# Bias masks for two key blocks at once in the tail rows, and one query load per head in the second half of the batch

## The chip, the cores and the metric

The kernel runs on one core of a Trainium2 chip. The metric is the device time of one execution in microseconds (us). The core has a matrix engine (PE, with its weight loads listed as PEld), a vector engine (DVE), a scalar engine (ACT), a general engine (POOL), and a queue (SP) from which all of this kernel's DMAs are issued. Each engine works through its instructions in the order in which they stand in its queue.

## What is computed

Attention with a learned relative bias, and then a two-layer network with a squared ReLU:

```python
# q, k, v: (4, 8, 576, 64); w1: (1, 32); b1: (32); w2: (32, 8)
scores = scale * np.matmul(q, k.transpose(0, 1, 3, 2))
psi_rel = np.log1p(np.abs(rel))                     # rel[i, j] = i - j
psi_i = np.log1p(np.maximum(pos[:, None], 1.0))
h = np.maximum((psi_rel / psi_i)[..., None] @ w1 + b1, 0.0)
scores = scores + (h @ w2).transpose(2, 0, 1)[None]
attn = np.exp(scores - max); attn = attn / (sum + 1e-09)
x = np.matmul(attn, v) as (2304, 512)
# network: w_in (512, 2048), w_out (2048, 512)
out = np.maximum(x @ w_in, 0.0) ** 2 @ w_out
```

## The kernel before

**Units.** The 576 query rows are cut into five chunks: four of 128 rows and a tail of 64 rows (`TAIL`, index 4). Heads go in pairs (`hp`, four of them). A unit is one batch, one pair of heads, one chunk. In the tail, the two heads of a pair share the 128 partitions, 64 rows each. The first 40 units are batches 0 and 1 (`b < AB`), by chunk: u0 to u7 are the tail chunk of the eight (batch, pair) combinations, u8 to u15 chunk 0, and so on. The last 40, u40 to u79, are batches 2 and 3, by (pair, batch), five chunks each, the tail last.

A unit runs `scores` (matmuls into the PSUM tile `sp`, then on DVE `t`, which adds the bias and takes the row extreme, then on ACT `p`, the exponential), two units later `transposes` (PE into `pp`, ACT copies to `pt`), then `values` (PE into `px`, copied to `xT`). `sp` has one buffer, `t` two, `p` three.

**Bias.** The bias of a chunk is made once, in 18 key blocks of 32 keys (`jb`), and is used by all batches. Because the bias is piecewise linear in the distance, `bias_mask` compares a window of a distance table with thresholds (`mask`, 128 partitions of 4 keys x 32 hidden units, 1024 two-byte elements each), and `bias_sum` multiplies the masks on PE by the weights `wmov` (16 matmuls per block, mask as the stationary operand of 128 columns, 64 columns moving) into a PSUM tile `bb`. ACT scales one half of it into `bt2`, DVE multiplies the other half by `xc` (the distances of that chunk, loaded by `load_xc`) into `bt1`, and POOL adds the two into `area`. In the tail a mask covers 64 rows and stands twice, for the two heads of a pair; for six of the 18 blocks (`MD`) DVE makes 64 columns and ACT copies them. The products are taken in two halves of 64 partitions. `bb`, `pp` and `px` share a ring of four PSUM buffers (`aux`), taken in the order of the program.

The tail's bias is made first. Between its blocks the program issues the loads of the eight (batch, pair) combinations of the first half, seven DMAs each: two of keys, four of queries (for each head the tail's 64 columns, L150, and the other 512, L151), one of values. After them it loads `xc` of chunk 0 (L573). The loop over units then makes `BO` blocks of the next chunk's bias beside the eight units of each chunk.

**The second half.** At unit 40 (`NA`) the loop loads keys and queries of the first three combinations of batches 2 and 3 (L637 to L639), then the first two of 16 tiles of `w_in` (`load_w`, L642 to L644, 512 KB each, two buffers). From unit 41 (`SC`) on, over ten units, each tile is scanned for its largest value (`scan_w`, DVE, L189) and the tile two further on is loaded into its buffer. The scans are held in program order on DVE. Later, `split_in` turns the tiles into pairs of two-byte parts beside the units, and then the network runs.

**Order.** The program is put into queues by a planner that simulates it with its own costs, so a change in one place can move instructions elsewhere.

Of the kernel before, what the change touches and what calls it, by code (L numbers as in the profile page):

```python
# [17 lines left out]
ALU = mybir.AluOpType  # L18
# [42 lines left out]
B1 = (2, 13, 8)  # L61
# [3 lines left out]
MD = 37449  # L65
K0 = 2
# [13 lines left out]
def attention_then_relu2_mlp(ctx: ExitStack, tc: tile.TileContext, q, k, v, cols, w_in, w_out, psi, xmat, dist, out):  # L80
# [65 lines left out]
    def load_q(b, hp):  # L146
        t = kq_p[-1].tile([128, S], F32, name="q1", tag="q1")
        for h in range(2):
            rows = slice(64 * h, 64 * h + 64)
            SP.dma_start(out=t[rows, 512:], in_=q[b, hp, TAIL, :, h, rows])  # L150
            SP.dma_start(out=t[rows, :512].rearrange("d (i m) -> d i m", i=TAIL), in_=q[b, hp, :TAIL, :, h].rearrange("i d m -> d i m"))  # L151
        q_t[b, hp] = t

# [182 lines left out]
    def bias_weights():  # L340
        ab = prep.tile([128, 2, H], F32, name="ab")
        part = prep.tile([128, 2, 2 * H], F16, name="part")
        eng = POOL if BW else DVE
        eng.memset(wmov, 0.0)
        for n in range(2):
            eng.tensor_scalar(out=ab[:, n], in0=col[:, 2:10], scalar1=(w1, b1)[n], scalar2=8.0, op0=ALU.mult, op1=ALU.mult)
        r = ab.rearrange("p a h -> p (a h)")

        pw = ps.tile([128, 512], F32, name="pw", tag="aux", bufs=4)
        sig, isig = power(r, pw[:, 0:1])  # L350
        eng.tensor_scalar(out=r, in0=r, scalar1=sig, scalar2=None, op0=ALU.mult)
        eng.tensor_copy(out=part[:, 0], in_=r)
        eng.tensor_tensor(out=part[:, 1], in0=r, in1=part[:, 0], op=ALU.subtract)
        wv = wmov.rearrange("p n (m j) -> p n m j", j=4)
        for jj in range(4):
            eng.tensor_copy(out=wv[32 * jj:32 * jj + 32, :, :, jj], in_=part[32 * jj:32 * jj + 32])
        return isig
# [3 lines left out]
    def bias_mask(ic, jb):  # L361
        m = prep.tile([128, 8, 128], F16, name="mask", tag="mask", bufs=MB)
        dup = ic == TAIL and (MD >> jb) & 1
        w = 64 if dup else 128
        base = sdist[:, 128 * ic + 548 - 32 * jb:]
        if ic < TAIL or dup:
            win = bass.AP(tensor=base.tensor, offset=base.offset, ap=[base.ap[0], [4, 8], [1, w]])
            th = theta[:, 128 * ic:128 * ic + w].unsqueeze(1)
            DVE.tensor_tensor(out=m[:, :, :w], in0=win, in1=th.to_broadcast([128, 8, w]), op=ALU.is_ge)  # L369
        else:  # L370
            win = bass.AP(tensor=base.tensor, offset=base.offset, ap=[base.ap[0], [4, 8], [0, 2], [1, 64]])
            th = theta[:, 512:].unsqueeze(1).unsqueeze(1).to_broadcast([128, 8, 2, 64])
            DVE.tensor_tensor(out=m.rearrange("p g (r i) -> p g r i", r=2), in0=win, in1=th, op=ALU.is_ge)
        if dup:
            ACT.copy(m[:, :, 64:], m[:, :, :64])
        mask_t[ic, jb] = m

    def bias_sum(ic, jb):
        m = mask_t.pop((ic, jb))
        bb = ps.tile([128, 512], F32, name="bb", tag="aux", bufs=4)  # L380
        for r in range(8):
            for n in range(2):
                PE.matmul(bb[:, 64 * (7 - r):64 * (8 - r)], lhsT=m[:, r], rhs=wmov[:, n], start=(n == 0), stop=(n == 1))  # L383
        t = prep.tile([128, H, 32], F32, name="bt1", tag="bt1", bufs=BB)
        s = prep.tile([128, H, 32], F32, name="bt2", tag="bt2", bufs=BB)
        xv = xc_t[ic][:, 32 * jb:32 * jb + 32].rearrange("p (g j) -> p g j", j=4).unsqueeze(1)
        bv = bb.rearrange("p (g a h j) -> p a h g j", g=8, a=2, h=H)
        tv = t.rearrange("p h (g j) -> p h g j", j=4)
        sv = s.rearrange("p h (g j) -> p h g j", j=4)
        js = slice(32 * jb, 32 * jb + 32)  # L390
        if ic < TAIL:
            ACT.activation(out=sv, in_=bv[:, 1], func=AF.Identity, scale=bscale)
# [4 lines left out]
            tw, sw = (y.rearrange("p (h e) j -> p h e j", e=2) for y in (t, s))  # L397
            POOL.tensor_tensor(out=dst, in0=tw, in1=sw, op=ALU.add)  # L398
        else:
            for r in range(2):  # L400
                rows = slice(64 * r, 64 * r + 64)
                bw = bb[rows].rearrange("p (g a h e j) -> p a e h g j", g=8, a=2, h=HP, e=2)
                ACT.activation(out=sv[rows, :HP], in_=bw[:, 1, r], func=AF.Identity, scale=bscale[rows])
                DVE.tensor_tensor(out=tv[rows, :HP], in0=bw[:, 0, r], in1=xv[rows].to_broadcast([64, HP, 8, 4]), op=ALU.mult)  # L404
            POOL.tensor_tensor(out=bias_t[:, 8::9, js], in0=t[:, :HP], in1=s[:, :HP], op=ALU.add)
# [4 lines left out]
    def scores(u):  # L410
# [11 lines left out]
        cols = slice(128 * ic, 128 * ic + 128 if ic < TAIL else S)  # L422

        for m, (x, h) in enumerate((x, h) for x in range(2) for h in (1, 0)):
            rows = slice(64 * h, 64 * h + 64)
            k0 = HALF * x + (64 if h and ic == TAIL else 0)
            out_t, to = (sps[h], slice(0, 128)) if ic < TAIL else (sps[0], rows)
# [114 lines left out]
    todo = [(ic, jb) for ic in chunks for jb in range(NJB)]  # L542
# [29 lines left out]
    bias_upto(NJB)  # L572
# [55 lines left out]
    for s in range(NU + TL + 1):  # L628
# [7 lines left out]
        for m, g in enumerate(groups[AB * HP:]):  # L636
            if s == max(first[g] - KL, NA):  # L637
                load_k(*g)
                load_q(*g)  # L639
            if s == max(first[g] - KL + TL + 1, NA - AB * HP + 2 + TL + m):  # L640
                load_v(*g)
        if s == SC - 1:  # L642
            load_w(ins[0])
            load_w(ins[1])  # L644
# [21 lines left out]
        if s < AB * HP * TAIL:  # L666
            n, r = divmod(s, AB * HP)
            bias_upto(NJB * (n + 1) + BO[r])
# [221 lines left out]
```

## Time and profile before

| | us |
|---|---|
| median of 3 runs | 798.25 |
| lowest, highest | 797.27, 798.29 |
| the profiled execution | 797.97 |
| its span from first to last instruction | 796.2 |

The profile is of one execution. Busy shares: PE 91%, PEld 72%, DVE 72%, ACT 57%, POOL 23%. Times in its views count from the start of the span, so what lies around the span is 1.77 us. The views used are the page's shares, the chain of work that ended last (each step followed back to what released it), timelines of one engine (start, length, line, operation, tiles and shapes, count, and in brackets the idle time before it with what ended it), sums by windows, and the list of waits. Matmul ends are modelled, so a group of many matmuls is read by the starts of what follows it. SPq is the issue of a DMA by the SP queue.

### The profile page before, as it was taken

The page shows a single profiled execution, that of the slowest core. Times are in us where ns is not written, and L with a number is a line of the kernel's source. Part 1 is how long each engine was busy: PE and PEld are TensorE (multiplying, and loading weights), DVE is VectorE, ACT ScalarE, POOL GpSimd, SP SyncE. Part 2 cuts the span into 40 slices and gives each one's busy share as a digit, 9 for nine tenths or more (in the row PEclk, how much of TensorE's full clock was granted, in tenths as well). Part 3 has the DMA queues.
Part 4 walks back from the last instruction along what each step waited for, and adds up shares of the span by engine and source line. Part 5 has one row for each costly group of instructions (what it writes and reads, how often), then busy time and mean ns, then how long its engine had stood idle before and what let it go on. Part 6 is the DMA issues. An engine that isn't in the chain of part 4 may idle for free.

```text
span 796.2 us, 17616 instructions
## 1 busy us (share of the span) xinstructions
PE 723.5 (91%) x7094; PEld 571.7 (72%) x7094; DVE 574.5 (72%) x1215; ACT 456.5 (57%) x940; POOL 186.4 (23%) x295
## 2 busy tenths in 40 slices
PE   5499999999988999979889899999989999999992
PEld 5456778787756676656677677878768887888881
DVE  7867778785666678898897979784845576557661
ACT  5757777777655678888676656664442233224220
POOL 1444333232210023342223324250400021000000
PEclk7869999999989999999999999999999999999997
DMA  7610000000376522301231143001010001000100
GB/s 203 191 60 18 3 16 2 3 2 2 105 239 232 189 85 85 111 28 54 80 107 54 67 146 107 28 22 59 26 54 1 1 1 54 1 1 1 54 2 27
DMA packets 27990, 50.14 MB, mean 63 GB/s; under 512 B 5252, under 2 KB 13444, under 8 KB 27908
## 3 DMA queue, kind: packets, MB, share of 16 engines
q1 hardware_dynamic: 27908, 49.01, 18.8%
q8 instruction: 56, 0.92, 0.5%
q14 instruction: 26, 0.21, 0.1%
HBM read 43.23 MB, written 5.77 MB: 62 GB/s over the span
## 4 chain that ended last, share of the span: by engine, by line
PE 50%; DVE 19%; ACT 8%; DMA 7%; SPq 6%; issue 5%; POOL 3%; DVEq 0%; ACTq 0%; POOLq 0%
PE y L766 16%; PE ha L717 8%; PE sp L428 7%; PE px L502 6%; PE hb L717 5%; PE pp L484 4%; PE bb L383 4%; DMA stage<-in_w_in 3%; DVE t L434 3%; ACT p L439 2%; SPq L150 2%; SPq L151 2%; DVE area L618 2%; DVE gl L747 1%; DVE wa L185 1%
## 5 line engine op out<-in xcount | busy, mean ns | idle before, releaser
L766 PE MATMUL y<-w,gh 128*128 128x512 f32 x576 | 177.9, 401 | 2.5 <-ACT gh L746 1.3
L717 PEld LDWEIGHTS <-area 128*128 128x128 f16 x1680 | 147.4, 99 | 42.5 <-issue 15.3
L439 ACT ACTIVATE p<-t,negm 128x576 f32<-128x576 f32 x144 | 111.2, 775 | 27.0 <-DVE negm L434 26.8
L434 DVE CUSTOM_DVE_ANT_0 t<-sp,area 128x576 f32<-128x576 f32 x144 | 104.1, 752 | 30.0 <-PE sp L428 21.3
L766 PEld LDWEIGHTS y<-w,gh 128*128 128x128 f32 x576 | 105.9, 190 | 24.9 <-ACT gh L746 2.9
L428 PE MATMUL sp<-k,q 64*128 64x288 f32 (+1 forms) x640 | 108.2, 447 | 15.0 <-DVE negm L434 11.4
L717 PE MATMUL ha<-area 128*128 128x256 f16 (+1 forms) x960 | 106.3, 266 | 9.0 <-DVE area L734 4.9
L766 PE MATMUL y<-w,gl 128*128 128x512 f32 x288 | 107.5, 397 | 1.1 <-DVE gl L747 1.1
L502 PE MATMUL px<-pt,v 128*64 128x128 f32 (+1 forms) x1600 | 96.6, 267 | 3.5 <-DVE xT L507 2.0
L485 ACT COPY pt<-pp 128x512 f32<-128x512 f32 x144 | 79.7, 582 | 32.0 <-PE pp L484 31.9
L502 PEld LDWEIGHTS px<-pt,v 128*64 128x64 f32 x1600 | 79.2, 137 | 19.7 <-issue 8.2
L484 PE MATMUL pp<-ident,p 128*128 128x128 f32 x576 | 84.5, 283 | 5.5 <-ACT pt L485 2.4
L428 PEld LDWEIGHTS sp<-k,q 64*128 64x128 f32 (+1 forms) x640 | 55.9, 182 | 41.1 <-DVE negm L434 15.3
L717 PE MATMUL hb<-area 128*128 128x256 f16 (+1 forms) x720 | 79.9, 262 | 1.4 <-DVE area L618 0.9
L484 PEld LDWEIGHTS pp<-ident,p 128*128 128x128 f32 x576 | 62.0, 142 | 22.8 <-issue 7.4
L398 POOL TENSOR_TENSOR area<-bt,bt 128x256 f32<-128x256 f32 x72 | 53.2, 763 | 81.9 <-DVE bt L393 81.9
L383 PE MATMUL bb<-wmov,mask 128*128 128x64 f16 x1440 | 52.6, 199 | 14.3 <-DVE bt L404 11.0
L766 PEld LDWEIGHTS y<-w,gl 128*128 128x128 f32 x288 | 53.8, 189 | 13.6 <-DVE gl L747 2.2
L383 PEld LDWEIGHTS <-mask 128*128 128x128 f16 x1440 | 48.2, 102 | 21.3 <-DVE bt L404 11.8
L369 DVE TENSOR_TENSOR mask<-sdist,theta 128x1024 f16<-128x1024 f16 (+1 forms) x78 | 49.7, 669 | 9.4 <-PE bb L383 9.4
L615 POOL TENSOR_TENSOR area<-xT 128x512 f32<-128x512 f32 (+1 forms) x17 | 22.8, 1344 | 143.2 <-DVE area L618 143.2
L747 DVE TENSOR_TENSOR gl<-area,gh 128x512 fp32r<-128x512 f32 (+1 forms) x40 | 30.2, 776 | 24.1 <-ACT gh L746 17.2
(153 smaller groups left out, 945.9 us busy)
## 6 DMA issues: line engine op xcount, KB each, us to landing
stage<-in_w_in SPq DMA_DIRECT2D x32, 512.0 KB, 4.2
stage<-in_w_out SPq DMA_DIRECT2D x16, 512.0 KB, 3.5
v<-in_v SPq DMA_DIRECT2D x16, 320.0 KB, 3.8
out<-o SPq DMA_DIRECT2D x18, 256.0 KB, 2.0
q<-in_q SPq DMA_DIRECT2D x32, 128.0 KB, 3.3
k<-in_k SPq DMA_DIRECT2D x16, 160.0 KB, 3.7
k<-in_k SPq DMA_DIRECT2D x16, 144.0 KB, 3.7
xc<-in_xmat SPq DMA_DIRECT2D x5, 288.0 KB, 3.6
```

What stands on the lines that cost most here:

```text
L369: DVE.tensor_tensor(out=m[:, :, :w], in0=win, in1=th.to_broadcast([128, 8, w]), op=ALU.is_ge)
L383: PE.matmul(bb[:, 64 * (7 - r):64 * (8 - r)], lhsT=m[:, r], rhs=wmov[:, n], start=(n == 0), stop=(n == 1))
L398: POOL.tensor_tensor(out=dst, in0=tw, in1=sw, op=ALU.add)
L428: mm = PE.matmul(out_t[to, x, :HALF], lhsT=qt[rows, cols], rhs=kt[rows, k0:k0 + HALF], start=True, stop=True)
L434: DVE.tensor_tensor_reduce(out=t.rearrange("p (x n) -> p x n", x=2), in0=sp[:, :, :HALF], in1=bias.rearrange("p (x n) -> p x n", x=2), sca ...
L439: ACT.activation(out=p[:, S * n:S * n + S], in_=t, func=AF.Exp, bias=negm[:, n:n + 1], scale=-1.0, accum_out=sums[:, 2 * ic + n:2 * ic + n ...
L484: PE.transpose(pp[:, 128 * c:128 * c + 128], p[:, k0:k0 + 128], ident)
L485: ACT.copy(pt[:, 4 * h:4 * h + 4], pp.rearrange("p (c m) -> p c m", c=4))
L502: PE.matmul(px[64 * h:64 * h + 64, :w], lhsT=vt[:, c, h], rhs=src, start=(c == 0), stop=(c == 4))
L717: PE.matmul(h[:, s, :w], lhsT=a, rhs=x, start=(k == 0), stop=(k == 5))
L747: DVE.tensor_tensor(out=gl, in0=g, in1=gh.bitcast(F32), op=ALU.subtract)
L766: PE.matmul(y, lhsT=a[:, slot, o:o + 128], rhs=x, start=((n, P) in firsts and f == 0 and m == 0), stop=((n, P) in lasts and f == 1 and m = ...
```

## The change

Three parts. In the tail, one mask now serves two key blocks: its 1024 elements are two narrow windows of 64 rows for neighbouring blocks, and nothing is doubled. The 18 blocks become nine pairs. Each narrow mask is loaded as a stationary operand of 64 columns, once for each head of a pair (`e`), into the upper or lower 64 partitions of `bb`, with 32 columns moving: 64 matmuls per pair of blocks in place of 32. The products on ACT and DVE and the add on POOL are then one operation per pair over all partitions. The order of heads in the weights changes to suit. In the second half, the queries of a head come in one DMA of 640 columns, the zero padding of the tail included, instead of two; `scores` reads the tail's columns at an offset for the second head. The first two loads of `w_in` are issued after the first and the second combination's keys and queries instead of after the third's. The counts `K0`, `B1` and the loop's targets are restated in pairs.

```diff
-B1 = (2, 13, 8)
+B1 = (2, 5, 8)
-MD = 37449
-K0 = 2
+K0 = 1
     def load_q(b, hp):
+        if b >= AB:
+            t = kq_p[-1].tile([128, NIC * 128], F32, name="q1", tag="q1")
+            for h in range(2):
+                SP.dma_start(out=t[64 * h:64 * h + 64].rearrange("d (i m) -> d i m", i=NIC), in_=q[b, hp, :, :, h].rearrange("i d m -> d i m"))
+            q_t[b, hp] = t
+            return
...
     def bias_mask(ic, jb):
...
+            base = sdist[:, 128 * ic + 548 - 32 * (jb + 1):]
+            win = bass.AP(tensor=base.tensor, offset=base.offset, ap=[base.ap[0], [4, 8], [32, 2], [1, 64]])
             th = theta[:, 512:].unsqueeze(1).unsqueeze(1).to_broadcast([128, 8, 2, 64])
+            out = m.rearrange("p g (x i) -> p g x i", x=2)
-        if dup:
-            ACT.copy(m[:, :, 64:], m[:, :, :64])
+        DVE.tensor_tensor(out=out, in0=win, in1=th, op=ALU.is_ge)
...
     def bias_sum(ic, jb):
...
-            for r in range(2):
-                rows = slice(64 * r, 64 * r + 64)
-                bw = bb[rows].rearrange("p (g a h e j) -> p a e h g j", g=8, a=2, h=HP, e=2)
-                ACT.activation(out=sv[rows, :HP], in_=bw[:, 1, r], func=AF.Identity, scale=bscale[rows])
-                DVE.tensor_tensor(out=tv[rows, :HP], in0=bw[:, 0, r], in1=xv[rows].to_broadcast([64, HP, 8, 4]), op=ALU.mult)
-            POOL.tensor_tensor(out=bias_t[:, 8::9, js], in0=t[:, :HP], in1=s[:, :HP], op=ALU.add)
+            wv = wmov.rearrange("p n (a e y) -> p n e a y", a=2, e=2)
+            for x in range(2):
+                for r in range(8):
+                    o = 256 * x + 32 * (7 - r)
+                    for n in range(2):
+                        for e in range(2):
+                            PE.matmul(
+                                bb[64 * e:64 * e + 64, o:o + 32].rearrange("p (a y) -> p a y", a=2),
+                                lhsT=m[:, r, 64 - 64 * x:128 - 64 * x], rhs=wv[:, n, e], start=(n == 0), stop=(n == 1),
+                            )
...
+            ACT.activation(out=sv.rearrange("p h (g j) -> p h g j", j=4), in_=bv[:, 1], func=AF.Identity, scale=bscale)
+            DVE.tensor_tensor(out=tv.rearrange("p h (g j) -> p h g j", j=4), in0=bv[:, 0], in1=xv.to_broadcast([128, HP, 16, 4]), op=ALU.mult)
+            POOL.tensor_tensor(out=bias_t[:, 8::9, 32 * jb:32 * jb + 64], in0=tv, in1=sv, op=ALU.add)
...
+            q0 = 128 * ic + (64 if h and ic == TAIL and b >= AB else 0)
+            cols = slice(q0, q0 + (128 if ic < TAIL else 64))
...
-    todo = [(ic, jb) for ic in chunks for jb in range(NJB)]
+    todo = [(ic, jb) for ic in chunks for jb in range(0, NJB, 2 if ic == TAIL else 1)]
...
             if s == max(first[g] - KL, NA):
                 load_k(*g)
                 load_q(*g)
+                if s == SC - 1 and m < 2:
+                    load_w(ins[m])
...
-        if s == SC - 1:
-            load_w(ins[0])
-            load_w(ins[1])
```

## Rows read from the trace of the kernel before

**Rows 1.** The page, part 1: busy us of each engine, share of span, instructions.
```profile
PE 723.5 (91%) x7094; PEld 571.7 (72%) x7094; DVE 574.5 (72%) x1215; ACT 456.5 (57%) x940; POOL 186.4 (23%) x295
```
**Rows 2.** Chain that ended last, 0 to 140 us: start, length, what.
```profile
2.59 0.59 SPq L137
...
40.27 0.60 SPq L143
40.92 3.62 DMA xc<-in_xmat
44.56 0.78 ACT xc L121
...
57.33 0.73 PE px L502 x20
58.06 1.51 PE bb L383 x48
```
**Rows 3.** Timeline of DVE, 0 to 50 us: the tail's masks, the first scores.
```profile
23.55 0.79 DVE L373 TENSOR_TENSOR mask<-sdist,theta 128x1024 f16<-128x1024 f16 x1
...
24.59 0.41 DVE L369 TENSOR_TENSOR mask<-sdist,theta 128x512 f16<-128x512 f16 x1
...
27.09 0.80 DVE L373 TENSOR_TENSOR mask<-sdist,theta 128x1024 f16<-128x1024 f16 x1
...
39.05 0.76 DVE L434 CUSTOM_DVE_ANT_0 t<-sp,area 128x576 f32<-128x576 f32 x1
```
**Rows 4.** Timeline of DVE, 44 to 100 us: products of chunk 0, first scores of u8.
```profile
46.07 1.08 DVE L393 TENSOR_TENSOR bt<-bb,xc 128x256 f32<-128x256 f32 x3
...
70.77 0.76 DVE L434 CUSTOM_DVE_ANT_0 t<-sp,area 128x576 f32<-128x576 f32 x1 [1.35 <-POOL area L398]
```
**Rows 5.** Timeline of PE, up to 207 us: bias products, scores, narrow stationary operands.
```profile
13.67 4.42 PE L383 MATMUL bb<-wmov,mask 128*128 128x64 f16 x80 [3.33 <-DVE wmov L356]
...
46.21 2.25 PE L428 MATMUL sp<-k,q 64*64 64x288 f32 x8 [0.97 <-DVE negm L434]
48.39 2.74 PE L383 MATMUL bb<-wmov,mask 128*128 128x64 f16 x48
...
56.14 1.19 PE L428 MATMUL sp<-k,q 64*64 64x288 f32 x8
...
204.67 0.41 PE L470 MATMUL ra<-rows,pick 27*64 27x128 bf16 x8
204.92 0.19 PE L470 MATMUL rt<-rows,pick 27*64 27x64 bf16 x2
```
**Rows 6.** Windows of 10 us: busy us (count) by engine, granted clock, DMA share, GB/s.
```profile
40.00:50.00 10.00, 8.17 (x55) 4.37 (x56) 4.63 (x12) 5.02 (x11) 3.44 (x7) 0.50 0.35 115
...
240.00:250.00 10.00, 7.97 (x87) 6.04 (x85) 6.57 (x19) 6.21 (x15) 0.97 (x5) 1.00 0.82 263
```
**Rows 7.** Timeline of the SP queue, 195 to 300 us: loads at unit 40 and after.
```profile
210.02 0.47 SPq L137 DMA_DIRECT2D k<-in_k  x1
...
211.18 0.60 SPq L150 DMA_DIRECT2D q<-in_q  x1
...
221.41 2.00 SPq L151 DMA_DIRECT2D q<-in_q  x1
223.51 1.02 SPq L172 DMA_DIRECT2D stage<-in_w_in  x2
...
263.88 1.73 SPq L150 DMA_DIRECT2D q<-in_q  x1
```
**Rows 8.** Timeline of DVE, 196 to 275 us: the first and the last scan.
```profile
227.74 0.69 DVE L189 TENSOR_REDUCE small<-stage 128x1 f32<-128x512 f32 x1 [3.60 <-DMA stage<-in_w_in]
...
269.96 0.69 DVE L189 TENSOR_REDUCE small<-stage 128x1 f32<-128x512 f32 x1 [1.46 <-DMA stage<-in_w_in]
```
**Rows 9.** Waits, 205 to 275 us: total us, times, longest.
```profile
DVE small L189 <- DMA stage<-in_w_in: 13.0, 10, 3.6
```
**Rows 10.** Chain that ended last, 140 to 420 us: a piece of `split_in`.
```profile
325.51 0.69 DVE zw L185
```

## What was predicted before the run

> **What bounds the kernel now.** The page's shares come first [rows 1]: PE is busy 91% of the span, so elsewhere a microsecond of another engine is mostly hidden. The change touches two stretches where PE is not the limit, so each is read for itself. For the first I read the chain of waits: from 2.59 to 40.9 us it runs through the issue of DMAs alone, 56 of them (8 combinations x 7) at about 0.65 us each, then through the load of `xc` for chunk 0, which lands at 44.54, and its scaling on ACT to 45.34 [rows 2]. Beside that chain DVE makes the tail's bias: three blocks repeat every 27.09 - 23.55 = 3.54 us, 1.18 us a block, and the first `t` runs at 39.05 [rows 3]. PE only runs in bursts there, and its granted clock is 0.50, the 1.2 GHz level, in the window from 40 to 50 us [rows 6]. From 48.39 PE works without a gap worth naming until u8's stage, where DVE's `t` stands at 70.77 [rows 4, 5]: that stretch is PE's.
>
> For the second I read SP's and DVE's timelines around unit 40. SP can issue from 210.02, when the memory of the first half's last unit is free, and needs until 223.4 for 18 loads of keys and queries; only then come the two loads of `w_in` [rows 7]. DVE stands still 3.60 us until the first has landed and scans it at 227.74; u42's `t` is queued behind that scan. The last scan is at 269.96 [rows 8]. In this stretch DVE waits 13.0 us for these loads [rows 9], and the DMA share is 0.82 at 240 to 250 us [rows 6]. It is a chain of loads into two buffers, not PE.
>
> **Tail's bias, work of each engine.** On DVE a pair of blocks cost 2 x 1.18 = 2.36 us. Now it costs one mask of 1024 elements, at most 0.79 [rows 3], and one product of 256 elements, 1.08 / 3 = 0.36 [rows 4]: 1.15. Nine pairs take 10.4 us in place of 21.2. The new window differs from the old wide one only in the step between its two halves, so I give it the same price. ACT loses six copies and three of every four products, POOL half its adds; neither was the limit and both get nothing.
>
> PE gets 576 matmuls in place of 288, each half as wide in stationary and moving columns. At 2.4 GHz a `bb` matmul takes 1.51 / 48 = 31.5 ns [rows 2]; half the moving columns, with two halves of the array side by side, would give 15.7 ns at the least. From above, `px` in the tail has the same stationary shape, also alternating between the halves, with 64 moving columns of four bytes: 0.73 / 20 = 36.5 ns [rows 2]. Nearest is `ra`, 64 two-byte stationary columns, alternating, 128 moving: 8 matmuls between the starts at 204.67 and 204.92, 31 ns [rows 5], and this one moves four times our columns. I take 24 ns, about midway between 15.7 and 31: 13.8 us (9.0 to 21.0). The first products ran at 4.42 / 80 = 55 ns, the lower clock level [rows 5]; those 4.4 us at half rate add 2.2. So the tail's bias is ready at 13.67 + 13.8 + 2.2 + 1.0 for the last product and add = 30.7 us (25.9 to 37.9), where `t` started at 39.05.
>
> **What that buys on the path.** Not 8 us, for the next thing late is `xc`: its load is behind the same 56 issues, so chunk 0's products still cannot start before 45.4. While they wait, their `bb` tiles hold all four `aux` buffers, and the first transposes stand behind them. With `p` three deep and `t` two, the tail units can get as far as p(u2), t(u4) and the score matmuls of u5. Before, they had got to p(u2), with sp(u3) at 46.21, right where chunk 0's work should have begun. So the gain is: the fifth `bb` can start at about 45.9 and not at 48.39, 2.5 us, and the score matmuls of u4 and u5 leave PE's gapless stretch, 2 x 1.19 = 2.4 [rows 5]. That is 4.9 at most; nothing at least, if the tail is ready only at 37.9 or if the planner does not use the window. I take 3.5, since DVE and ACT share the stretch and will not follow PE to the last. The time at u8 then carries over, as PE is full up to unit 40.
>
> **The loads at unit 40.** The order becomes: two loads of keys, two of queries, `w_in` 0, the same again, `w_in` 1, then the third combination. The first `w_in` load is issued after four issues of about 0.6 us, at 210.02 + 2.5 = 212.5 in before's time, not at 223.51: 11 us sooner [rows 7]. With the landing it took before (223.51 to 227.74, 4.2 us) it is there at 216.7; if the keys' and queries' traffic doubles that, at 221. Either is before DVE is free for it at about 224.1, which is 227.74 less the 3.60 of idling. What is moved behind it, the third combination's keys and queries, needs six fewer issues in all and still goes out by about 218.5 instead of 223.4; its units come ten units later. Nobody waits for that. The first scan, and with it u42's `t` and the load into the freed buffer, comes 3.6 us earlier (0 to 4.2). The 15 steps to the last scan took 269.96 - 227.74 = 42.2 us, 2.8 us each, paced by two buffers; I keep that pace. The first step also had a part that waited for the second tile, which now is there too: 0.6 more, so 4.2.
>
> **Query loads.** Each of the eight combinations saves two issues, 1.2 us of SP. In the first half nothing changes, since `load_q` branches on `b >= AB`. Late in the scans two query loads stand right ahead of the last tile's load, one of them 1.73 us [rows 7]. One issue of 0.6 us leaves that place: 0.6 (0 to 2.3). The 32 KB of padding for each combination is 256 KB, at 263 GB/s [rows 6] 1 us of traffic spread over 130 us: nothing.
>
> **The sum.** 3.5 + 4.2 + 0.6 = 8.3 us. Against the profiled execution: 797.97 - 8.3 = 789.7. The median of the runs is 0.3 above that execution, so 790.0. From the bounds alone: best 4.9 + 4.2 + 2.3 = 11.4, so 786.9; worst 798.25.
>
> **Rivals.** First, the tail's gain stays behind the load of `xc`: the planner lets DVE and PE wait in the same places as now, or the narrow matmuls cost 36.5 ns and the tail is ready at 37.9. Then 4.8 us remain, 793.5. For it: 45.34 is fixed by 56 issues that nothing shortens. Against it: sp(u3) demonstrably sat on PE at 46.21. It decides from a tail that is ready at 38, 1 us short of 39.05: (38 - 16.9) / 576 = 37 ns per matmul. The Trainium skill says in "TensorEngine Tiling (Array Packing)", under Restrictions, that column tiling switches off the fast weight load, and in "TensorE: Matmul & The Clock Gate", under LDWEIGHTS, that a load takes its columns / 1.2 in ns. By that, an estimate of 53 ns for 64 columns, the loads alone would take 31 us if the two halves' loads did not overlap, the tail would be ready near 47, and this rival would hold; `ra`'s 31 ns per matmul speaks for an overlap.
>
> Second, the scans are bound by bandwidth and not by their start: the share of 0.82 means that whatever lands earlier delays something else, and the last scan stays near 269. Then only 3.5 + 0.6 remain, 794.2. Against it: the 11 us ahead of the scans carry less traffic than that.
>
> Third, on the slower side: the planner places the pieces of `split_in` and `split_x` otherwise after 271 us, where PE is not full and DVE, ACT and POOL hand work to one another. A piece such as 0.69 us on DVE [rows 10] that moves ahead of a unit's `t` puts off the unit by as much. From 8.3 / 0.69 = 12 such places on it eats the gain; 15 of the 29 units from u51 on would be 10.4 us, so 790.0 + 10.4 = 800.4. For it: the planner sees new costs and new loads, and orders by its own model. Against it: that part of the program is the same, and it only starts earlier.
>
> Fourth, both gains fail and the change does nothing that counts: about 798.
>
> **How the numbers follow.** Forecast 0.47, first rival 0.18, second 0.14, third 0.12, fourth 0.09. The time is the likeliest's, 790.0. The range from 785.5 to 797.5 takes in the first two rivals and the best sum with some room for an order that happens to fit better; it leaves out the third and most of the fourth. A measurement of this kernel can tell about 0.2%, 1.6 us, from no change. The forecast and the first two rivals are faster, 0.79; within 0.2%: 0.09; slower: 0.12.
>
> **What would show it.** In the changed kernel's timelines: nine masks and nine products on DVE in the tail; the first `t` near 31 us; 64 narrow matmuls of a pair in about 1.5 us at the 2.4 GHz level; `xc` landing still near 44.5; PE's `bb` work starting again by 46 and u8's `t` near 67. Around unit 40, counted from SP's first key load: `w_in` 0 issued 2.5 us after it instead of 13.5, the first scan without its 3.6 us of waiting, the last scan about 55 us after that load instead of 60. From there on the stretch to the end should have the old length, about 526 us. The prediction is wrong if the matmuls take over 37 ns, if u8's `t` does not move, or if the last stretch changes its length by more than 2 us.

## The result and the profile after

The changed kernel is slower: median 803.33 us (802.03 to 807.0, six runs) against 797.34 us for the kernel before (795.53 to 798.29, six runs), ratio 1.0086, 95% interval 1.0067 to 1.0106. The profiled execution took 803.9 us, its span is 802.1 us, 5.9 more than before. Runs of one kernel spread by about 0.6% either way, so verdicts below go by ratios, and a trace, which is of one run, is used for where the time lies.

The page's shares [rows 1] hardly differ, and so don't tell where the 6 us lie:

```profile
PE 728.8 (91%) x7382; PEld 579.6 (72%) x7382; DVE 565.5 (70%) x1179; ACT 442.7 (55%) x907; POOL 185.7 (23%) x286
```

I therefore laid the two traces side by side by units: the first `t` of each unit on DVE's timeline, after minus before. That gives +10.2 us at u0, +7.1 at u8, +2.9 from u17 to u39, -0.7 at u50, +5.4 at u53 and the same to u79, +5.9 at the end. Three stretches thus have a sign of their own: **+2.9 up to u39, -3.7 from u39 to u50, +6.1 from u50 to u53**; the rest adds 0.6.

**Up to u39.** Timelines of the changed kernel at the end of the tail's bias: ACT (products of `bb`, scaling of `xc`), then DVE, then POOL:

```profile
29.15 0.48 ACT L411 ACTIVATE bt<-bb,small 128x256 f32<-128x256 f32 x1 [1.23 <-PE bb L403]
45.95 0.78 ACT L120 ACTIVATE xc<-xc,small 128x576 f32<-128x576 f32 x1 [16.33 <-DMA xc<-in_xmat]
46.63 0.45 ACT L411 ACTIVATE bt<-bb,small 128x256 f32<-128x256 f32 x1
...
47.12 0.42 DVE L412 TENSOR_TENSOR bt<-bb,xc 128x256 f32<-128x256 f32 x1 [15.04 <-ACT bt L411]
49.21 0.74 DVE L443 CUSTOM_DVE_ANT_0 t<-sp,area 128x576 f32<-128x576 f32 x1
...
30.19 0.74 POOL L413 TENSOR_TENSOR area<-bt,bt 128x256 f32<-128x256 f32 x1 [0.97 <-DVE bt L412]
47.62 1.11 POOL L413 TENSOR_TENSOR area<-bt,bt 128x256 f32<-128x256 f32 x1 [16.69 <-DVE bt L412]
```

Eight of nine pairs are added by 30.9. The ninth pair's product (L411, 46.63) stands behind the scaling of chunk 0's `xc` (L120) in ACT's queue. That scaling waits 16.3 us for the load, and with it wait the last product, DVE, POOL and every unit. In the kernel before, this scaling, at 44.56 [rows 2], stood behind the first exponentials, as its timeline of ACT shows:

```profile
40.17 0.78 ACT L439 ACTIVATE p<-t,negm 128x576 f32<-128x576 f32 x1
...
44.56 0.78 ACT L121 ACTIVATE xc<-xc,small 128x576 f32<-128x576 f32 x1 [0.73 <-DMA xc<-in_xmat]
```

In the changed program too it comes behind all of the tail's products; the planner put it in front of the last one.

**At unit 40.** SP's timeline, first loads, against [rows 7]:

```profile
212.95 0.47 SPq L136 DMA_DIRECT2D k<-in_k  x1
213.47 0.59 SPq L137 DMA_DIRECT2D k<-in_k  x1
214.10 1.68 SPq L149 DMA_DIRECT2D q<-in_q  x2
215.88 0.56 SPq L172 DMA_DIRECT2D stage<-in_w_in  x1
...
261.16 0.49 SPq L136 DMA_DIRECT2D k<-in_k  x1
261.71 0.59 SPq L137 DMA_DIRECT2D k<-in_k  x1
262.34 0.62 SPq L149 DMA_DIRECT2D q<-in_q  x1
263.37 0.33 SPq L172 DMA_DIRECT2D stage<-in_w_in  x1
263.75 0.62 SPq L149 DMA_DIRECT2D q<-in_q  x1
264.63 7.58 SPq L172 DMA_DIRECT2D stage<-in_w_in  x3
```

`w_in` 0 goes out 2.9 us after the first key load (before: 13.5), and the first scan runs at 226.51 without a wait. The last six lines hold the last two tiles (263.37 and 264.63), now 1.3 us apart and between the keys and queries of the fifth combination. In before they were issued 3.1 us apart, 262.65 and 265.71. DVE's timeline shows the last two scans [rows 8], PE's, below them, who waits:

```profile
269.42 0.69 DVE L189 TENSOR_REDUCE small<-stage 128x1 f32<-128x512 f32 x1 [3.20 <-DMA stage<-in_w_in]
271.16 0.69 DVE L189 TENSOR_REDUCE small<-stage 128x1 f32<-128x512 f32 x1 [0.86 <-DMA stage<-in_w_in]
...
270.36 2.40 PE L511 MATMUL px<-pt,v 128*64 128x128 f32 x20 [2.75 <-DVE xT L516]
273.80 2.29 PE L437 MATMUL sp<-k,q 64*128 64x288 f32 x8 [1.03 <-DVE small L217]
```

Windows of 5 us of the same stretch, columns as in [rows 6]:

```profile
265.00:270.00 5.00, 2.60 (x22) 1.74 (x17) 1.80 (x5) 2.75 (x7) 0.98 (x5) 0.95 0.90 240
270.00:275.00 5.00, 3.60 (x26) 3.01 (x28) 3.06 (x12) 1.63 (x4) 0.00 (x0) 0.50 0.66 210
275.00:280.00 5.00, 5.00 (x34) 3.67 (x31) 1.88 (x8) 2.27 (x6) 0.00 (x0) 0.52 0.04 13
280.00:285.00 5.00, 5.00 (x50) 3.54 (x48) 1.87 (x6) 2.26 (x6) 0.00 (x0) 1.00 0.00 0
```

The clock falls within PE's first wait (2.75 us, up to 270.36): the granted clock is 0.95 from 265 to 270 and then 0.50, the 1.2 GHz level, in the two windows from 270 to 280. The second wait (1.03 us) lies in that stretch. The matmul groups behind the waits take 2.40 and 2.29 us; in the kernel before, the groups of the same lines take 1.31 (at 269.53) and 1.24 (at 268.36). DVE's waits on the loads of `w_in` sum to 7.4 us from 205 to 275, where they were 13.0 [rows 9]: less in all, but now more than half of it at the last two scans.

The start of the last scan (271.16, before 269.96) divides the 6.1 us. Windows from u50's `t` to the last scan, and from there to u53's `t`, first of the kernel before, then of the changed one:

```profile
265.57:269.96 4.39, 4.39 (x50) 3.40 (x50) 2.32 (x8) 3.47 (x10) 0.00 (x0) 1.00 0.81 264
269.96:277.92 7.96, 6.79 (x78) 5.12 (x73) 5.01 (x20) 4.96 (x13) 0.00 (x0) 1.00 0.31 107
```
```profile
264.84:271.16 6.32, 3.55 (x33) 2.68 (x31) 2.27 (x7) 2.75 (x7) 0.99 (x5) 0.87 0.78 207
271.16:283.28 12.12, 11.09 (x74) 8.00 (x72) 4.92 (x19) 5.23 (x13) 0.00 (x0) 0.64 0.26 86
```

Up to the last scan 1.9 us are lost, in PE's wait. Behind it 4.2 us are lost: PE is busy for 11.09 us in place of 6.79 with about as many matmuls, at a mean clock of 0.64 in place of 1.00, and idle for no longer than before.

### The profile page after: what moved, and what is told of

It is laid out like the page before. It is cut to its first block, busy times and chain, and to the rows that moved or that the text cites. A ratio compares the mean times of both kernels' runs of the same rounds, so it can differ in the third digit from the quotient of the medians.

```text
span 802.1 us, 18086 instructions
## 1 busy us (share of the span) xinstructions
PE 728.8 (91%) x7382; PEld 579.6 (72%) x7382; DVE 565.5 (70%) x1179; ACT 442.7 (55%) x907; POOL 185.7 (23%) x286
## 4 chain that ended last, share of the span: by engine, by line
PE 56%; DVE 17%; DMA 6%; ACT 6%; SPq 5%; issue 5%; POOL 2%; DVEq 0%; ACTq 0%; POOLq 0%
PE y L774 18%; PE ha L725 8%; PE sp L437 7%; PE px L511 7%; PE pp L493 5%; PE hb L725 5%; PE bb L384 4%; DVE t L443 3%; DMA stage<-in_w_in 3%; DVE area L627 2%; SPq L156 1%; DMA stage<-in_w_out 1%; SPq L155 1%; ACT p L448 1%; DVE gl L755 1%
## 5 line engine op out<-in xcount | busy, mean ns | idle before, releaser
L437 PE MATMUL sp<-k,q 64*128 64x288 f32 (+1 forms) x640 | 104.3, 437 | 8.9 <-DVE negm L443 5.5
L511 PE MATMUL px<-pt,v 128*64 128x128 f32 (+1 forms) x1600 | 98.7, 271 | 5.0 <-DVE xT L516 2.7
L511 PEld LDWEIGHTS px<-pt,v 128*64 128x64 f32 x1600 | 81.1, 139 | 21.2 <-issue 7.4
L373 DVE TENSOR_TENSOR mask<-sdist,theta 128x1024 f16<-128x1024 f16 x81 | 56.0, 727 | 14.4 <-PE bb L403 8.2
L774 PEld LDWEIGHTS y<-w,gl 128*128 128x128 f32 x288 | 53.4, 188 | 13.5 <-DVE gl L755 2.2
L384 PE MATMUL bb<-wmov,mask 128*128 128x64 f16 x1152 | 42.3, 198 | 14.8 <-DVE mask L373 14.2
L384 PEld LDWEIGHTS <-mask 128*128 128x128 f16 x1152 | 38.4, 101 | 20.4 <-DVE mask L373 15.5
L755 DVE TENSOR_TENSOR gl<-area,gh 128x512 fp32r<-128x512 f32 (+1 forms) x40 | 30.7, 786 | 25.3 <-ACT gh L754 18.3
```

Of the source, the lines that this page charges most:

```text
L373: DVE.tensor_tensor(out=out, in0=win, in1=th, op=ALU.is_ge)
L437: mm = PE.matmul(out_t[to, x, :HALF], lhsT=qt[rows, cols], rhs=kt[rows, k0:k0 + HALF], start=True, stop=True)
L511: PE.matmul(px[64 * h:64 * h + 64, :w], lhsT=vt[:, c, h], rhs=src, start=(c == 0), stop=(c == 4))
L755: DVE.tensor_tensor(out=gl, in0=g, in1=gh.bitcast(F32), op=ALU.subtract)
L774: PE.matmul(y, lhsT=a[:, slot, o:o + 128], rhs=x, start=((n, P) in firsts and f == 0 and m == 0), stop=((n, P) in lasts and f == 1 and m = ...
```

## The experiments

Two claims are put to the test: that ACT's order, or `xc`'s late load, cost the tail its gain; and that the loss from u50 to u53 comes of the loads, by way of PE's clock. The table gives all kernels: the ratio to before with its interval; from one profiled run, the first `t` of a unit and the end of the span, each minus before; the time from u50's `t` to u53's; and the lowest granted clock of a 5-us window between them.

| kernel | ratio | u0 | u8 | u39 | u50 | u53 | end | u50 to u53 | clock |
|---|---|---|---|---|---|---|---|---|---|
| before | 1 | 0 | 0 | 0 | 0 | 0 | 0 | 12.35 | 1.00 |
| after | 1.0086 (1.0067 to 1.0106) | +10.2 | +7.1 | +2.9 | -0.7 | +5.4 | +5.9 | 18.44 | 0.50 |
| tail_only | 1.0043 (1.0017 to 1.0069) | +10.2 | +7.4 | +3.3 | +1.0 | +1.8 | +2.8 | 13.21 | 1.00 |
| loads_only | 1.0062 (1.0026 to 1.0099) | +0.4 | -0.7 | -0.7 | -5.4 | +0.8 | -1.1 | 18.53 | 0.50 |
| w_only | 1.0006 (0.9987 to 1.0025) | +0.6 | -0.6 | -0.4 | -1.4 | +0.3 | +0.2 | 14.12 | 0.70 |
| q_only | 1.0047 (1.0020 to 1.0073) | +0.1 | -1.1 | -1.0 | -3.1 | +1.6 | +1.5 | 17.11 | 0.51 |
| act_c | 1.0035 (1.0007 to 1.0063) | -4.1 | -0.9 | +0.5 | +1.6 | +6.3 | +5.8 | 17.04 | 0.50 |
| xc_early_pin | 0.9985 (0.9963 to 1.0007) | -3.8 | -6.5 | -10.5 | -13.5 | -7.7 | -2.9 | 18.13 | 0.50 |
| before_xc_early_pin | 0.9903 (0.9869 to 0.9936) | +1.5 | -4.0 | -8.4 | -10.0 | -7.4 | -8.6 | 15.00 | 0.76 |
| loads_xc | 0.9957 (0.9936 to 0.9978) | +2.5 | -3.4 | -7.7 | -9.6 | -4.7 | +1.4 | 17.31 | 0.59 |
| tail_xc | 0.9857 (0.9835 to 0.9879) | -3.2 | -5.9 | -10.2 | -10.9 | -10.6 | -10.2 | 12.66 | 1.00 |
| tail_xc_q | 0.9970 (0.9947 to 0.9993) | -3.7 | -6.5 | -10.2 | -12.5 | -8.2 | -1.7 | 16.69 | 0.50 |
| late_kq | 1.0074 (1.0041 to 1.0108) | +9.6 | +6.6 | +2.3 | -1.7 | +3.5 | +3.6 | 17.64 | 0.55 |
| xc_early_late | 0.9973 (0.9950 to 0.9996) | -3.0 | -5.8 | -9.8 | -9.9 | -8.8 | -6.5 | 13.51 | 0.71 |
| no_kq | 0.9981 (0.9957 to 1.0006) | +9.4 | +6.4 | +2.5 | -0.8 | -0.6 | -0.9 | 12.50 | 1.00 |
| fill6 | 1.0071 (1.0046 to 1.0097) | +9.8 | +6.8 | +2.8 | +2.2 | +2.9 | +8.6 | 13.01 | 1.00 |

**The two parts apart: tail_only, loads_only.** Each undoes one half of the change:

```diff
 # tail_only: the loads of before
-        if b >= AB:
-            t = kq_p[-1].tile([128, NIC * 128], F32, name="q1", tag="q1")
...
-                if s == SC - 1 and m < 2:
-                    load_w(ins[m])
+        if s == SC - 1:
+            load_w(ins[0])
+            load_w(ins[1])
```
```diff
 # loads_only: the bias of before, whole
-B1 = (2, 5, 8)
+B1 = (2, 13, 8)
...
```

> The change's tail bias with the loads of before (query loads and w_in's place as before). Theory (the loss ahead of unit 40 and the one behind unit 50 are separate, the first by the tail, the second by the loads): first t near 49 as in the changed kernel, +2.9 us from unit 17 to unit 40, and the same +2.9 at unit 50 and at the end, so about 800.5 to 801.5, 3 us over before. Rival (the planner answers the tail's new costs and new due times by another order behind unit 50, and that is the large loss): the jump of 5 to 6 us between units 50 and 53 stays although the loads are those of before, and the time is about 806.

> The change's loads with the tail bias of before. Theory: units 0 to 40 as in before within 0.3 us; first scan without its 3.6 us of waiting, so unit 50 about 3.6 us sooner than before; then w_in's last two tiles land late behind the keys and queries issued at unit 50, and 5 to 6 us are given back by unit 53: in all +1 to +3 us, about 799 to 800.5. Rival (the jump between units 50 and 53 comes with the tail's new order): no jump, the gain of 3.6 us stays, about 794.

The two losses are separate, as the theory said of both. The tail alone loses 3.3 us by u39 and has no jump behind u50; the loads alone gain 4.7 us from u39 to u50 and give back 6.2 by u53. Of the tail's 3.3, 1.8 are left by u53, which the theory had not expected. Most of what it wins back lies between u40 (+3.3) and u46 (+1.0), where the clock of the kernel before was at 0.50 from 230 to 235 us and that of tail_only stayed at 1.00; whether that is the cause was not tested. The median of tail_only, 800.44 us, is just under its theory's range, that of loads_only, 801.48, over it. The profile of loads_only is of the fastest of its six runs (797.0).

**ACT's order and the load of `xc`: act_c, xc_early_pin, before_xc_early_pin.** The first holds chunk 0's scaling behind the tail's products, chunk 0's three products there and the first exponential. The second leaves the scaling where the program has it and loads `xc` earlier; the third does that to the kernel before.

```diff
 # act_c
-        if ic != chunks[0]:
+        if ic not in chunks[:2]:
             scale_xc(ic)
...
             scores(s)
+        if s == 0:
+            scale_xc(chunks[1])
 # xc_early_pin, before_xc_early_pin: ahead of the loop that loads batch 1
+    load_xc(chunks[1])
     for b in range(1, AB):
...
-    load_xc(chunks[1])
 # all three, in scale_xc
+        if ic in chunks[1:3]:
+            tc.keep_in_program_order(ins)
```

> The changed kernel; only the scaling of chunk 0's xc on ACT is put behind the tail's last product, chunk 0's three products there and the first exponential. Theory (the tail's last pair is held on ACT by that scaling, which waits for xc's load until 45.95, and with it the first t): tail complete near 33, first t near 33 to 35 instead of 49.21, u8's t at 71 or earlier instead of 77.86, so the 2.9 us up to unit 40 vanish or turn into a gain of up to 3.5; with the loss behind unit 50 unchanged the time is 797 to 800.5, 3 to 6 us under the changed kernel. Rival (the narrow matmuls and the low clock level set the start, not ACT's queue): the first t may come sooner, but u8's t stays near 78 and the time near 803.

> The changed kernel; only chunk 0's xc is loaded ahead of the keys and queries of batch 1 (one load moved in SP's queue, some 35 to 40 issues forward), with the scaling on ACT kept at its place in the program, so chunk 0's work need not wait for 45. Theory (xc's load behind SP's issues is what keeps the tail's gain from the path): xc lands near 25 to 30, the first t near 33, and chunk 0's products follow at once; PE's gapless stretch begins up to 10 us sooner, u8's t near 67 to 70; time 796 to 799. Rival (PE at the low clock level is the limit there once it has work, so an earlier xc buys nothing beyond the order on ACT): same as with the scaling moved, within 1 us of that kernel.

> The kernel before, with chunk 0's xc loaded ahead of batch 1's keys and queries, its wide tail bias and its loads as they were. In the changed kernel the same move put unit 39 10.5 us ahead of before (13.5 ahead of the changed kernel). Theory (both are needed: the tail of before is ready only at 39, so an early xc lets chunk 0's products follow a tail that is itself late): first t near 39, u8's t at 67 to 69 instead of 70.77, unit 39 by 2 to 5 us sooner, time 793 to 796. Rival (xc alone was the gate, the narrow masks are worth little): unit 39 by 8 or more us sooner, time 790 or less.

Timelines of ACT and DVE in act_c:

```profile
32.29 0.48 ACT L413 ACTIVATE bt<-bb,small 128x256 f32<-128x256 f32 x1 [1.82 <-PE bb L405]
45.01 0.78 ACT L120 ACTIVATE xc<-xc,small 128x576 f32<-128x576 f32 x1 [7.39 <-DMA xc<-in_xmat]
...
34.95 0.74 DVE L445 CUSTOM_DVE_ANT_0 t<-sp,area 128x576 f32<-128x576 f32 x1
45.82 1.09 DVE L392 TENSOR_TENSOR bt<-bb,xc 128x256 f32<-128x256 f32 x3 [8.00 <-ACT xc L120]
```

The first `t` is at 34.95, so ACT's order did hold the tail: theory right there, and at u8, whose `t` is at 69.90 where the rival had it near 78. But only 2.4 us of it reach u39 (+0.5 in place of +2.9), and nothing of a gain: DVE stands 8.00 us before chunk 0's products, until `xc` has landed and is scaled. The time, 801.11 us, lies over the theory's range: behind u39 this run was slower than the changed kernel's, with a low clock (0.83) at 230 to 240 as well. Timelines of SP, ACT and DVE in xc_early_pin:

```profile
21.87 0.43 SPq L115 DMA_DIRECT2D xc<-in_xmat  x1
...
30.14 0.77 ACT L120 ACTIVATE xc<-xc,small 128x576 f32<-128x576 f32 x1
...
35.27 0.74 DVE L445 CUSTOM_DVE_ANT_0 t<-sp,area 128x576 f32<-128x576 f32 x1
```

One load issued at 21.87 in place of 42.75, with its scaling held at its place in the program, moves u39 from +2.9 to -10.5, 13.5 us. The time, 794.81 us, is below the theory's 796 to 799. In the kernel before the same move gives 8.4 us at u39 and the ratio 0.9903, more than the 2 to 5 us of its theory: its rival, that `xc` was the gate, is right. The narrow masks are worth 1.8 us at u39 with the loads of before (tail_xc below, against before_xc_early_pin) and 2.8 with those of the change (xc_early_pin against loads_xc below), and only once `xc` is there: no run had them gain without it.

**Which part of the loads: w_only, q_only.** The kernel before with one of the two parts:

```diff
 # w_only
+                if s == SC - 1 and m < 2:
+                    load_w(ins[m])
 # q_only
+        if b >= AB:
+            t = kq_p[-1].tile([128, NIC * 128], F32, name="q1", tag="q1")
...
```

> The kernel before, with w_in's first two tiles between the loads of the first three combinations, and the four query loads per combination as before. Theory (w_in's order gives the gain at the first scans, and the loss behind unit 50 comes of the earlier keys there, not of the query loads' form): first scan with less than 1 us of waiting, unit 50 2 to 5 us sooner, and the jump of 4 us or more between units 51 and 53 is there as well, end within 1.5 us of before. Rival (the padded query tiles, 32 KB more each, make the late tiles late): no jump, unit 53 and the end 2 to 5 us sooner than before.

> The kernel before with the change's query loads (two per combination in the second half, padded) and w_in's first two tiles where they were, behind the third combination. With both parts of the loads unit 50 was 5.4 us sooner and unit 53 0.8 later; with w_in's new place alone unit 50 was 1.4 sooner and unit 53 0.3 later. Theory (the query loads bring the earlier start, since six issues fewer stand ahead of w_in's first tile, and with it the jump behind unit 50): SP issues w_in's first tile 3 to 4 us sooner than before, unit 50 2 to 4 us sooner, unit 53 within 1 us of before, end within 1.5 us. Rival (each part is worth what it saves, and only both together press the last tiles together): unit 50 and the end both 2 to 4 us sooner than before.

From u39 to u50, w_in's new place gains 1.0 us, the query loads 2.1, both 4.7, more than the sum. In w_only the first scan no longer waits, but the third waits 4.57 us for its tile, where it waits 1.65 in loads_only. Of the loss from u50 to u53 (12.35 before), w_only has 1.8, q_only 4.8, both together 6.2. The query loads carry most of either sign, so the theory for w_only failed in size: it had 2 to 5 us at u50 and a jump of 4 or more. That for q_only held up to u50 (-3.1), but not its 1 us at u53 (+1.6).

**The loss behind u50: late_kq, no_kq, fill6.** The first loads the last four combinations' keys and queries two units later in the program; the second doesn't load them; the third puts six matmuls of ones behind unit 51's scores.

```diff
 # late_kq
-            if s == max(first[g] - KL, NA):
+            if s == max(first[g] - KL + 2 * (m >= 4), NA):
 # no_kq
+                if m >= 4:
+                    p = groups[AB * HP + 3]
+                    k1_t[g], q_t[g] = k1_t[p], q_t[p]
+                    continue
 # fill6, in scores
+        if u == 51:
+            for _ in range(6):
+                mm = PE.matmul(sp4[:, 0, 352:480], lhsT=ones, rhs=ones, start=True, stop=True)
+                tc.keep_in_program_order(mm)
```

> The changed kernel; the keys and queries of the last four combinations are loaded two units later each, so those issued at unit 50 no longer stand between w_in's last tiles. Theory (w_in's last two tiles share the DMA engines with them, land 6 us after issue, PE waits for the units behind the scans and its clock falls): the last scan at about 267 to 268.5 instead of 271.16, u53's t at 278 to 280 instead of 283.28, time 4 to 6 us under the changed kernel, 797 to 799.5. Rival (PE idles there and its clock falls whatever the order, since the two buffers pace the scans): the last scan may move by 1 to 2 us, u53's t stays at 282 or later, time 801 or more.

> The changed kernel without the keys and queries of the last four combinations: they are not loaded, and the units of these combinations use the tiles of the fourth of the second half (so this part of the scores is computed from other data). From unit 45's loads on, SP's queue holds w_in's and w_out's tiles alone. The kernel with those loads two units later in the program did not tell: on SP's queue they stood at the same places ahead of w_in's last two tiles. Theory (these loads delay w_in's last two tiles): landing 4 to 4.7 us after issue instead of 6.05 and 6.5, the last scan at 267 to 268.5 instead of 271.16, u53's t at 277.5 to 280 instead of 283.28, time 797 to 799.5. Rival (the scans are paced by two buffers and by DVE's order; PE's wait and the fall of its clock come wherever the scans end): last scan 269.5 or later, u53's t 282 or later, time 801 or more.

> The changed kernel with six matmuls of ones behind the score matmuls of unit 51, into columns of that PSUM tile that nobody reads: work of about 1.4 us at 2.4 GHz in the 2.75 us in which PE waits at 267.6 to 270.36. Nothing waits less for it. Theory (of the 6.1 us lost from unit 50 to unit 53 some 4 are the fall of the clock after that wait): the granted clock stays at 1.00 from 265 to 280, u53's t 10 to 11 us behind u50's instead of 18.4... that is at 279 instead of 283.28, time 798 to 799.5. Rival (the wait on the scans is the loss, the low clock is hidden beside it): the clock row may change, u53's t stays at 282 or later, time 801 or more.

late_kq tells nothing of its question: on SP's queue those loads stood around w_in's last two tiles as before, and the jump stayed. Without the loads (no_kq) it is gone: u50 to u53 takes 12.50 us, and the ratio falls from 1.0086 to 0.9981. The last scan, at 269.34, came only 1.8 us sooner than in the changed kernel, less than the theory's 2.7 and near the rival's bound, but PE's waits differ and the clock does not fall; u53's `t`, at 277.30, and the time, 796.74 us, are just below the theory's ranges. PE's timeline of no_kq behind the last scan, and the window from that scan to u53's `t`:

```profile
270.95 0.35 PE L198 MATMUL pw<-small,ones 128*128 128x1 f32 x2 [1.99 <-DVE small L218]
272.35 1.24 PE L437 MATMUL sp<-k,q 64*128 64x288 f32 x8 [0.45 <-DVE negm L443]
```
```profile
269.34:277.30 7.96, 5.90 (x59) 4.48 (x61) 5.01 (x20) 4.96 (x13) 0.00 (x0) 1.00 0.33 114
```

The same two views of fill6 (the group of ones is the added work; its count is of passes, two a matmul):

```profile
270.51 1.60 PE L442 MATMUL sp<-ones 128*128 128x128 f32 x12
274.47 0.35 PE L198 MATMUL pw<-small,ones 128*128 128x1 f32 x2 [1.12 <-DVE small L218]
```
```profile
272.86:280.82 7.96, 6.40 (x69) 4.73 (x67) 5.01 (x19) 4.95 (x13) 0.00 (x0) 1.00 0.44 131
```

In fill6 the last scan is at 272.86, later than in the changed kernel, and yet from it to u53's `t` takes 7.96 us, as in the kernel before: the loss behind the last scan is the clock's, and does not come of a late scan. The table's 13.01 us from u50 to u53 flatters the run, since u50's `t` itself came 3.0 us later than in the changed kernel; from u39 to u53 it is 2.3 us shorter, not 5.4. u53's `t`, at 280.82, lies between the theory's 279 and the rival's 282, and the time, 804.16 us, is the rival's: 5.7 us were lost behind u53, 4.3 of them from u70 to u79. The six matmuls also moved other instructions (PE's waits there became shorter), so the run doesn't prove that filling the wait kept the clock up.

Across all kernels, the five traces without a fall take 12.35 to 13.21 us from u50 to u53, and all five 7.95 or 7.96 from the last scan on; the eleven with one take 13.51 to 18.53, and 9.31 to 12.23 from the last scan on. So the fall is shown to cost 4.2 us in the changed kernel. What brings it is less clear: no_kq takes away the issues and the bytes of those loads together. Ten of the eleven have a part of the change's loads, but before_xc_early_pin has none and shows a short fall too (0.76). Nor does the distance of the last two tiles decide: they are issued 1.25 us apart in no_kq, without a fall, and 3.1 in xc_early_late, with one.

**All parts with the early `xc`: loads_xc, tail_xc, tail_xc_q, xc_early_late.** The early load of xc_early_pin on loads_only, on tail_only, on tail_only with the query loads, and on late_kq.

> The kernel before with the change's loads and with chunk 0's xc loaded ahead of batch 1's keys and queries; the wide tail bias of before. Theory (the loads' loss between units 50 and 53 is theirs alone): unit 39 by 8.4 us sooner, unit 50 by 11 to 13, unit 53 by 6 to 8, end 789 to 792, 1 to 3 us over the kernel with the early xc and the loads of before. Rival (the loss came with the narrow bias's order): end 784 to 787.

> The change's tail bias with the loads of before, and chunk 0's xc loaded ahead of batch 1's keys and queries, its scaling kept at its place. With the wide bias of before and the same move of xc, unit 39 was 8.4 us sooner than before and the end 8.65 us sooner (span 787.5); with the changed kernel and the same move unit 39 was 10.5 us sooner and the end 2.9. Theory (the narrow masks are worth what they save once xc no longer gates, and the loads take it back later): unit 39 by 10.5 us sooner, end by 9.5 to 11, time 786 to 788. Rival (another 2 us at unit 40 are waited out in the scans or the network): unit 39 by 10.5 us, end by 8.7 or less, time 789 or more.

> The narrow tail bias, chunk 0's xc loaded early, the change's query loads, and w_in's first two tiles where they were in before. The same kernel with the old query loads ended 10.2 us sooner than before (span 786.0). Theory (the query loads alone do not press w_in's last tiles against keys and queries): 784 to 787. Rival (the query loads bring the jump behind unit 50 as they did with w_in's new place): 789 to 793.

> The changed kernel with both repairs: chunk 0's xc loaded ahead of batch 1, and the keys and queries of the last four combinations two units later. Theory (two losses that add up): unit 39 10.5 us ahead of before as with the early xc alone, no jump between units 50 and 53, so 4 to 5 us under the early xc alone: 789 to 791. Rival (what is won before unit 53 is waited out in the network, where the early xc alone already lost 2.6 us from unit 71 on): unit 53 sooner by 5 us, the end by 2 at most, 793 or more.

tail_xc beats both kernels: 787.98 us, ratio 0.9857 (0.9835 to 0.9879), as its theory had it. Two windows, then the last two scans on DVE:

```profile
250.00:260.00 10.00, 9.47 (x98) 6.46 (x94) 6.18 (x17) 4.99 (x13) 1.22 (x6) 1.00 0.78 227
260.00:270.00 10.00, 8.56 (x89) 6.33 (x89) 5.97 (x24) 6.87 (x18) 0.00 (x0) 1.00 0.29 95
```
```profile
257.56 0.69 DVE L185 TENSOR_REDUCE small<-stage 128x1 f32<-128x512 f32 x1 [1.45 <-DMA stage<-in_w_in]
259.38 0.69 DVE L185 TENSOR_REDUCE small<-stage 128x1 f32<-128x512 f32 x1 [0.94 <-DMA stage<-in_w_in]
```

The two waits are 1.45 and 0.94 us in place of 3.20 and 0.86, and the clock stays. Adding the query loads to it (tail_xc_q) brings back the fall and 0.0113 of the ratio: the rival is right about the jump, though 795.29 us is over its range. The last two scans wait 1.31 and 1.10 us there, much as in tail_xc, so these two waits do not decide the fall. loads_xc shows the same from the other side: 0.0054 over the early `xc` alone. The jump stays with the wide bias, as its theory had it, but the time, 795.82 us, is over its 789 to 792; its trace lost another 6 us behind u79, in a run 3.6 us over its median. xc_early_late (794.66 us, in the rival's range) kept the order on SP as late_kq did, so its gain over xc_early_pin (0.0012, intervals overlap) is no evidence.

## Why the prediction was wrong

- **Tail's bias, each engine's work: right on DVE, right on PE by luck.** Nine masks and nine products on DVE; eight of nine pairs added at 30.9 against 30.7 for all. The price of a narrow matmul was put at 24 ns (15.7 to 36.5) at the 2.4 GHz level and is 27 to 28 ns at the lower one, from PE's timeline:

```profile
13.73 8.64 PE L403 MATMUL bb<-wmov,mask 128*64 128x32 f16 x316 [4.73 <-DVE wmov L356]
22.77 3.60 PE L403 MATMUL bb<-wmov,mask 128*64 128x32 f16 x128 [0.40 <-issue]
27.05 3.60 PE L403 MATMUL bb<-wmov,mask 128*64 128x32 f16 x128 [0.68 <-issue]
```

  8.64 / 316 = 27.3 and 3.60 / 128 = 28.1 ns. All of it ran at the 1.2 GHz level; the prediction had that level for 4.4 us only. The two errors cancel; the price at 2.4 GHz was not measured. By the Trainium skill ("TensorE: Matmul & The Clock Gate", LDWEIGHTS) a weight load takes its columns / 1.2 in ns, an estimate of 53 ns for 64 columns. The trace has two matmuls, one in each half, every 55 ns, so by that figure the loads of the halves overlapped, as `ra` had suggested.
- **"ACT loses six copies ..., neither was the limit and both get nothing": failed.** ACT's queue took the scaling of `xc` between the eighth and ninth pair. That one instruction in another place put u0 10.2 us later; act_c shows it.
- **What that buys on the path, 3.5 (0 to 4.9): failed, and the lower bound with it.** Measured +2.9 us at u39. Put right on ACT alone it is +0.5: the first rival (the gain stays behind `xc`) was the truth of the mechanism, and 0.18 was too little for it. The prediction had read the gate itself, 56 issues ahead of `xc` [rows 2]; what the runs add is its price, 8.4 us in the kernel before.
- **Loads at unit 40, 4.2: right at the first scan, wrongly shared out.** Counted from the first key load the first scan came at 226.51 - 212.95 = 13.6 us instead of 17.7, 4.2 sooner. The pace was to stay 2.8 us a scan; it became (271.16 - 226.51) / 15 = 3.0, so the last scan is 58.2 us behind that load, not 55. That goes part of the way to the second rival (transfers delay one another), by which it would have stayed near 60. By u50, 3.7 us of 4.8 were there. The query loads, priced at 0.6, carry two thirds of what the parts gain alone.
- **"From there on the stretch to the end should have the old length, about 526 us": failed.** It is 802.1 - 271.2 = 530.9, 4.7 us longer, where the prediction had named 2 us as a sign of being wrong. This is the largest term missing from the sum: PE waited for the scans of the last two tiles, and its clock fell for 10 us. Of 18.44 - 12.35 = 6.1 us, 1.9 lie ahead of the last scan, where PE waits, and 4.2 behind it, where the clock is low. No rival had it, though the kernel before showed the same fall behind its wait at the first scan (0.50 from 230 to 235, 0.68 over 230 to 240). The prediction costed that wait at its length alone.
- **Third rival, pieces of the network in other places after 271: not here.** From u53 to the end the change adds 0.6 us. The planner's order mattered, but on ACT ahead of u0. It did cost 4.3 us from u70 to u79 in fill6 and 2.6 in xc_early_pin; what moved there was not followed up.

The sum as measured: +2.9 - 3.7 + 6.1 + 0.6 = +5.9, for -3.5 - 4.2 - 0.6.

## What to carry to other kernels

Before pricing work that ends sooner, list what its consumer also waits for, and move that first: here one load, 20 us sooner in SP's queue, was worth more than the whole change (0.9903 alone, 0.9857 with the narrow masks). Where a planner orders the queues, look for instructions that wait for a late DMA and could be put ahead of the work that is made faster. A wait on PE is priced with what the clock does behind it: here 1.9 us lost by waiting were followed by 4.2 us lost to slower matmuls. And loads that start sooner are not worth their earlier start by themselves: on top of the narrow masks and the early `xc`, the old loads are better than the new ones by 0.0128 of the ratio (tail_xc against xc_early_pin).

## What the runs showed of the hardware

Over 20 to 30 us the kernel before had PE busy for less than half the time at the full clock, and the changed kernel had it busy for nine tenths at the low one. The windows, before first, then after:

```profile
20.00:30.00 10.00, 4.36 (x132) 3.96 (x129) 9.21 (x26) 7.67 (x21) 4.74 (x9) 1.00 0.69 201
```
```profile
20.00:30.00 10.00, 8.92 (x328) 8.70 (x326) 5.14 (x11) 2.38 (x5) 3.69 (x5) 0.50 0.56 158
```

PE's busy share as the profile counts it therefore does not tell the granted clock; narrow matmuls kept PE busy for 17 us without bringing the 2.4 GHz level back. Likewise 3.0 idle us in five (PE busy 1.97 of 5) left the clock at 1.00 in tail_only at 230 to 235 us, and 3.0 in five (busy 2.01) in before at 225 to 230 were followed by 0.50. What decides between them stays open.
